# Statistics of one token tile moved from VectorE to ScalarE, and two copies halved between the engines, at the start of a layer-norm, state-space and gated-unit kernel

## The chip, the cores and the metric

One NeuronCore of a Trainium2 chip. The metric is device microseconds of one execution, median over the executions of a kernel. The span in a trace is about 1.9 us shorter than that time.

## The reference, cut to what matters

```python
def _layernorm(x, axis=-1, eps=1e-5):
    m = jnp.mean(x, axis=axis, keepdims=True)
    v = jnp.var(x, axis=axis, keepdims=True)
    return (x - m) / jnp.sqrt(v + eps)
...
    x  = A_x                      # 1 x 2048 x 576, bf16
    xn = _layernorm(x, axis=-1)
    return x + _A_ref(xn, ...) + _B_ref(xn, B_w_gate, B_w_up, B_w_down)
# _B_ref: (sigmoid(xn @ w_gate) * (xn @ w_up)) @ w_down, 576 -> 4608 -> 576
# _A_ref: a diagonal complex state space over the 2048 tokens
```

## The kernel before

Tokens are processed in tiles of 128 (tile 0, 1, 2, ...), four tiles to a block of 512. Nothing can be multiplied until the first tiles are normalised and transposed, so the start is a chain across all engines. For a tile: VectorE takes statistics of its two halves and aggregates them, ScalarE takes the square root, VectorE the reciprocal and the normalisation, TensorE 18 transposes into PSUM (where TensorE leaves its results), and ScalarE and VectorE copy the result out (9 chunks of 128 columns) into `xT`. Then the first gate/up group `start_groups[0]` can run on tiles 0 and 1, before tiles 2 and 3 are transposed.

```python
    busy(10, TB)               # warm-up matmuls on zeros, 512 columns
    busy(6, P)                 # and 128 columns
    ...
    for tt in range(2):
        ln_stats(tt)                                   # VectorE: 2 halves + aggregate
        ln_std(0, tt, tt + 1)                          # ScalarE: square root
    for tt in range(2):
        ln_recip(0, tt, tt + 1)                        # VectorE
        ln_norm(tt, twice=False)                       # VectorE
        start_transpose(tt)                            # TensorE
    consts_transpose(ptrs[1][:, NH, :])
    busy(18, P)
    start_copy(0, slice(0, NH), nc.scalar.copy)
    ln_stats(2)
    start_copy(1, slice(0, 5), nc.scalar.copy)
    ln_std(0, 2, 3)
    ln_stats(3)
    ln_std(0, 3, 4)
    start_copy(1, slice(5, NH), nc.vector.tensor_copy)
    for tt in range(2, TT_B):
        ln_recip(0, tt, tt + 1)
        ln_norm(tt, twice=False)
    start_groups[0].mms(slice(0, 2 * P))               # TensorE: tiles 0 and 1
    start_transpose(2)
    start_transpose(3)
    start_groups[1].mms(slice(0, 2 * P))               # from here on TensorE never waits
    # ... copies of tiles 2 and 3, second halves of both groups, then the steady loop
```

The order of these lines is the order of instructions on each engine. In the traces here every engine takes its own in that order: in e4 and e12 below TensorE stands for one instruction while the work of later ones is ready.

## Time and profile before

| | before |
|---|---|
| time, median of 3 (lowest to highest) | 506.17 us (506.12 to 506.29) |
| time of the execution that was profiled | 506.76 us, span 504.9 |
| first statistics of tile 0 start (tile 0 has landed) | 3.49 us |
| first transpose, tile 0 | 6.27 us |
| first gate/up group | 9.03 us |
| transposes of tile 2 | 10.29 us |
| steady stream starts | 11.45 us |

The positions are starts read from the trace. From the order of time on ScalarE and VectorE (start, duration, engine, line, operation, what it writes and reads, and in brackets the idle time before it and what ended it):

```profile
7.26 1.71 ACT L783 COPY xT<-ptr 128x1152 bf16<-128x1152 bf16 x2 [1.46 <-PE ptr L780]
```
```profile
8.20 0.21 DVE L231 BATCH_NORM_AGGREGATE mv<-bnst 128x2 f32<-128x12 f32 x1
9.01 0.42 DVE L783 COPY xT<-ptr 128x512 bf16<-128x512 bf16 x1 [0.60 <-ACT xT L783]
```

ScalarE's two copies one after the other take 1.71 us; VectorE has finished the statistics of tile 3 and waits 0.60 us for them. The change goes after that wait.

### The profile page before, as it was taken

The page shows a single profiled execution, that of the slowest core. Times are in us where ns is not written, and L with a number is a line of the kernel's source. Part 1 is how long each engine was busy: PE and PEld are TensorE (multiplying, and loading weights), DVE is VectorE, ACT ScalarE, POOL GpSimd, SP SyncE. Part 2 cuts the span into 40 slices and gives each one's busy share as a digit, 9 for nine tenths or more (in the row PEclk, how much of TensorE's full clock was granted, in tenths as well). Part 3 has the DMA queues.
Part 4 walks back from the last instruction along what each step waited for, and adds up shares of the span by engine and source line. Part 5 has one row for each costly group of instructions (what it writes and reads, how often), then busy time and mean ns, then how long its engine had stood idle before and what let it go on. Part 6 is the DMA issues. An engine that isn't in the chain of part 4 may idle for free.

```text
span 504.9 us, 13370 instructions
## 1 busy us (share of the span) xinstructions
PE 500.5 (99%) x5892; PEld 290.6 (58%) x5892; DVE 323.3 (64%) x706; ACT 204.7 (41%) x368; POOL 91.0 (18%) x134
## 2 busy tenths in 40 slices
PE   8999999999999999999999999999999999999997
PEld 6544675444477444467764444774444774446775
DVE  5889698887878687886688767696675222221111
ACT  4955733556500756530016655005655005553000
POOL 7116320123100043110001231100431001300000
PEclk9999999999999999999999999999999999999999
DMA  8997595055220099340340651200643201600001
GB/s 210 208 176 232 135 197 100 18 149 139 49 50 26 1 160 215 73 95 26 90 101 4 162 142 49 49 25 1 165 106 84 50 25 34 179 1 1 26 25 49
DMA packets 40960, 45.77 MB, mean 91 GB/s; under 512 B 28614, under 2 KB 32326, under 8 KB 40902
## 3 DMA queue, kind: packets, MB, share of 16 engines
q0 software_dynamic: 10608, 34.22, 27.8%
q1 hardware_dynamic: 29862, 10.37, 11.1%
q8 instruction: 46, 0.75, 0.6%
q10 hardware_dynamic: 432, 0.33, 0.2%
q14 instruction: 12, 0.10, 0.1%
HBM read 34.36 MB, written 2.36 MB: 73 GB/s over the span
## 4 chain that ended last, share of the span: by engine, by line
PE 99%; DVE 0%; ACT 0%; issue 0%
PE pgu L502 55%; PE pd L616 33%; PE pbu L531 7%; PE pd L576 1%; PE pd L584 1%; PE pgu L772 1%; PE ptr L780 0%; ACT xT L783 0%; DVE xn L255 0%; DVE xT L783 0%; DVE ob L585 0%; DVE warm L182 0%; DVE rstd L238 0%; DVE eps_t L178 0%; DVE zero_t L180 0%
## 5 line engine op out<-in xcount | busy, mean ns | idle before, releaser
L502 PE MATMUL pgu<-xT,wgu 64*128 64x512 bf16 (+1 forms) x2628 | 283.7, 373 | 0.1
L502 PEld LDWEIGHTS <-wgu 64*128 64x128 bf16 x2628 | 128.1, 94 | 150.4
L616 PE MATMUL pd<-wd,hT 64*128 64x288 bf16 x2208 | 140.5, 283 | 0.0
L508 ACT ACTIVATE sT<-pgu 128x512 bf16<-128x512 f32 x144 | 86.3, 600 | 120.5 <-PE pgu L502 119.6
L616 PEld LDWEIGHTS <-hT 64*128 64x128 bf16 x2208 | 107.6, 94 | 28.7
L511 DVE TENSOR_TENSOR hT<-sT,uT 128x512 bf16<-128x512 bf16 x144 | 60.6, 422 | 91.5 <-ACT uT L509 91.3
L509 ACT CAST uT<-pgu 128x512 bf16<-128x512 f32 x144 | 84.0, 583 | 0.0
L154 POOL DMA_DIRECT2D wgu<-in_B_w_gate_dram x36 | 27.6, 766 | 227.7 <-PE pgu L502 216.3
L537 ACT COPY bure<-pbu 128x512 f32<-128x512 f32 x16 | 9.4, 585 | 89.9 <-PE pbu L531 76.0
L160 POOL DMA_DIRECT2D wd<-in_B_w_down_dram x36 | 26.3, 733 | 104.9 <-PE pd L616 104.7
L627 DVE TENSOR_TENSOR acc<-acc,pd 128x576 f32<-128x576 f32 x32 | 22.7, 750 | 30.2 <-PE pd L616 30.2
L624 DVE TENSOR_TENSOR ob<-acc,pd 128x576 bf16<-128x576 f32 x14 | 9.9, 750 | 38.3 <-PE pd L616 38.3
L531 PE MATMUL pbu<-xT,bt 64*128 64x512 bf16 x288 | 33.7, 376 | 0.0
L616 PE MATMUL pd<-ctim,hst 64*128 64x288 bf16 x224 | 28.6, 283 | 0.0
L616 PE MATMUL pd<-ctre,hst 64*128 64x288 bf16 x224 | 28.6, 283 | 0.0
L616 PEld LDWEIGHTS <-hst 64*128 64x128 bf16 x504 | 24.5, 94 | 6.3
L154 POOL DMA_DIRECT2D wgu<-in_B_w_up_dram x36 | 26.5, 736 | 1.5 <-DMA wgu<-in_B_w_up_dram 1.5
L445 DVE TENSOR_TENSOR_SCAN gre<-r,g0re,wrim 128x512 bf16<-128x512 f32 x20 | 25.5, 1277 | 0.1
L531 PEld LDWEIGHTS <-bt 64*128 64x128 bf16 x288 | 14.0, 94 | 16.5
L452 DVE TENSOR_TENSOR_SCAN gim<-r,g0im,wrim 128x512 bf16<-128x512 f32 x16 | 20.4, 1275 | 0.0
L230 DVE BATCH_NORM_STATS2 bnst<-xt 128x6 f32<-128x288 bf16 x32 | 12.5, 432 | 2.3 <-DMA xt<-in_A_x_dram 2.3
L432 DVE TENSOR_TENSOR tq<-T,buim 128x512 bf16<-128x512 bf16 x20 | 13.7, 684 | 0.0
(126 smaller groups left out, 294.6 us busy)
## 6 DMA issues: line engine op xcount, KB each, us to landing
wgu<-in_B_w_gate_dram POOLq DMA_DIRECT2D x36, 288.0 KB, 4.2
wgu<-in_B_w_up_dram POOLq DMA_DIRECT2D x36, 288.0 KB, 4.8
wd<-in_B_w_down_dram POOLq DMA_DIRECT2D x36, 288.0 KB, 4.7
out_dram<-ob SPq DMA_DIRECT2D x15, 144.0 KB, 1.7
xt<-in_A_x_dram SPq DMA_DIRECT2D x10, 144.0 KB, 3.9
xt<-in_A_x_dram POOLq DMA_DIRECT2D x4, 144.0 KB, 6.8
bt<-ctre POOLq DMA_DIRECT2D x2, 288.0 KB, 6.0
bt<-ctim POOLq DMA_DIRECT2D x2, 288.0 KB, 7.7
```

The source lines that it names most:

```text
L154: eng.dma_start(w[rows, :, :], src[:, fs].rearrange("(c p) f -> p c f", p=H))
L160: nc.gpsimd.dma_start(wd[:], B_w_down[f0:f0 + FP * P, :].rearrange("(n p) d -> p n d", p=P))
L432: nc.vector.tensor_mul(tq[:], t2, b[:])
L445: nc.vector.tensor_tensor_scan(gre[:], r_bc, w[:, 0, :], g0re[:, col], ALU.mult, ALU.add)
L452: nc.vector.tensor_tensor_scan(gim[:], r_bc, w[:, 1, :], g0im[:, col], ALU.mult, ALU.add)
L502: nc.tensor.matmul(self.ps[:, gi, cols], w[rows, c, fs], xT[self.nb][rows, c, cols], start=c == 0, stop=c == NH - 1)
L508: nc.scalar.activation(sT[:], self.ps[:, 0, :], ACT.Sigmoid)
L509: nc.scalar.copy(uT[:], self.ps[:, 1, :])
L511: nc.vector.tensor_mul(h[:], sT[:], uT[:])
L531: nc.tensor.matmul(out, w, xT[self.nb][rows, c, ts_], start=c == 0, stop=c == NH - 1)
L616: m = nc.tensor.matmul(pds[k][:, a, 0:DH], lhsT[rows, :], rhs[rows, a * DH:(a + 1) * DH], start=turn == 0 and i == 0, stop=turn == 1 and i ...
L627: nc.vector.tensor_add(halves(acc[:]), halves(acc[:]), pd[:, :, 0:DH])
```

## The change

Its intent: take the statistics of tile 1 off VectorE, so that tiles 0, 2 and 3 come earlier there, and divide the copies of tiles 0 and 1 so that they overlap. The two runs of short warm-up matmuls are cut too, from 6 to 3 and from 18 to 6. ScalarE gets the mean from one accumulating pass (Identity, scale 1/576) and the variance from a second (Square of mean minus x); the second pass gives a sum, so the square root takes it with a scale of 1/576. Cuts in the diff are marked "...".

```diff
-    busy(6, P)
+    busy(3, P)
@@
+    m1, v1 = (mvs_of(0)[:, 1, i:i + 1] for i in range(2))
+    junk = [...]                                   # two scratch tiles
+    nc.scalar.activation(junk[1][:, 0:1], eps_t[:], ACT.Sqrt, ...)      # loads the table early
+    ln_stats(0)
+    nc.scalar.activation(junk[0][:], xts[1][:], ACT.Identity, bias=zero_t[:], scale=1.0 / D, accum_out=m1)
+    ln_std(0, 0, 1)
+    nc.scalar.activation(junk[1][:], xts[1][:], ACT.Square, bias=m1, scale=-1.0, accum_out=v1)
+    nc.scalar.activation(rstds[0][:, 1:2], v1, ACT.Sqrt, bias=eps_t[:], scale=1.0 / D)
+    ln_bn(2, 0)                                    # first half of tile 2's statistics
+    ln_recip(0, 0, 1)
+    ln_norm(0, twice=False)
+    start_transpose(0)
+    ln_bn(2, 1)
+    ln_recip(0, 1, 2)
+    ln_norm(1, twice=False)
+    start_transpose(1)
+    consts_transpose(ptrs[1][:, NH, :])
+    busy(6, P)
+    ln_aggr(2)
+    ln_bn(3, 0)
     for tt in range(2):
-        ... (the old order, shown above)
-    busy(18, P)
-    ...
+        start_copy(tt, slice(0, 4), nc.scalar.copy)
+        start_copy(tt, slice(4, NH), nc.vector.tensor_copy)
     ln_std(0, 2, 3)
-    ln_stats(3)
+    ln_bn(3, 1)                                    # behind the copies
+    ln_aggr(3)
     ln_std(0, 3, 4)
-    start_copy(1, slice(5, NH), nc.vector.tensor_copy)
     for tt in range(2, TT_B):
         ln_recip(0, tt, tt + 1)
         ln_norm(tt, twice=False)
```

`ln_bn` and `ln_aggr` are the two parts of `ln_stats`; nothing after these lines is changed.

More of the change, by code (lines that the diff above doesn't have):

```diff
@@ L220, with mvs_of, ln_bn, ln_aggr @@
     ln_count = [0]
-    def ln_stats(tt):
-        nb, tl = divmod(tt, TT_B)
-        if tl == 0:
+    bnst = {}
+    def mvs_of(nb):
+        if nb not in mvs:
             mvs[nb] = lnp.tile([P, TT_B, nc.vector.BN_AGGR_DIM], FP32, name="mv")
             rstds[nb] = lnp.tile([P, TT_B], FP32, name="rstd")
-        xt = xts[tt]
-        st = lnp.tile([P, 2, BN], FP32, name="bnst")
+        return mvs[nb]
+    def ln_bn(tt, gi):
+        if gi == 0:
+            bnst[tt] = lnp.tile([P, 2, BN], FP32, name="bnst")
+        nc.vector.bn_stats(bnst[tt][:, gi, :], xts[tt][:, gi * DH:(gi + 1) * DH])
+    def ln_aggr(tt):
+        nb, tl = divmod(tt, TT_B)
+        nc.vector.bn_aggr(mvs_of(nb)[:, tl, :], bnst[tt][:])
+    def ln_stats(tt):
         for gi in range(2):
-            nc.vector.bn_stats(st[:, gi, :], xt[:, gi * DH:(gi + 1) * DH])
-        nc.vector.bn_aggr(mvs[nb][:, tl, :], st[:])
+            ln_bn(tt, gi)
+        ln_aggr(tt)
     def ln_std(nb, t0, t1):
@@ L783, in start_copy @@
         eng(xT_tile(0)[:, cs, tt * P:(tt + 1) * P], ptrs[tt % 2][:, cs, :])
-    for tt in range(2):
-        ln_stats(tt)
-        ln_std(0, tt, tt + 1)
-    for tt in range(2):
-        ln_recip(0, tt, tt + 1)
-        ln_norm(tt, twice=False)
-        start_transpose(tt)
-    consts_transpose(ptrs[1][:, NH, :])
-    busy(18, P)
-    start_copy(0, slice(0, NH), nc.scalar.copy)
-    ln_stats(2)
-    start_copy(1, slice(0, 5), nc.scalar.copy)
+    m1, v1 = (mvs_of(0)[:, 1, i:i + 1] for i in range(2))
+    junk = [ssmp.tile([P, D], BF16, name="junk", tag="tq", bufs=2) for _ in range(2)]
+    nc.scalar.activation(junk[1][:, 0:1], eps_t[:], ACT.Sqrt, bias=zero_t[:], scale=1.0)
+    ln_stats(0)
[15 more added lines that the diff above has]
+    ln_bn(3, 0)
+    for tt in range(2):
+        start_copy(tt, slice(0, 4), nc.scalar.copy)
+        start_copy(tt, slice(4, NH), nc.vector.tensor_copy)
     ln_std(0, 2, 3)
-    ln_stats(3)
+    ln_bn(3, 1)
+    ln_aggr(3)
     ln_std(0, 3, 4)
-    start_copy(1, slice(5, NH), nc.vector.tensor_copy)
     for tt in range(2, TT_B):
```

## The prediction

> **What bounds the kernel now**
>
> I read the page first, for the engine that sets the end.
>
> ```profile
> PE 500.5 (99%) x5892; PEld 290.6 (58%) x5892; DVE 323.3 (64%) x706; ACT 204.7 (41%) x368; POOL 91.0 (18%) x134
> ...
> PE 99%; DVE 0%; ACT 0%; issue 0%
> ...
> L502 PE MATMUL pgu<-xT,wgu 64*128 64x512 bf16 (+1 forms) x2628 | 283.7, 373 | 0.1
> ...
> L616 PE MATMUL pd<-wd,hT 64*128 64x288 bf16 x2208 | 140.5, 283 | 0.0
> ```
>
> TensorE is the chain that ends last, and its two large groups sat idle 0.1 and 0.0 us. From the first steady gate/up matmuls on, nothing but TensorE counts: a change in the first 12 us is worth exactly the time by which that stream starts earlier, in a span of 504.9 us. So the second view is the chain cut to the first 32 us.
>
> ```profile
> 1.25 5.09 PE pgu L772 x16
> 6.34 0.90 PE ptr L780 x16
> 7.24 0.02 issue
> 7.26 1.72 ACT xT L783 x2
> 8.99 0.02 issue
> 9.01 0.42 DVE xT L783
> 9.44 0.08 DVE rstd L238
> 9.52 0.03 issue
> 9.54 0.71 DVE xn L255
> 10.25 0.04 issue
> 10.29 1.23 PE ptr L780 x36
> 11.52 20.53 PE pgu L502 x215
> ```
>
> Read downwards: warm-up matmuls until 6.3, the transposes of tiles 0 and 1, two ScalarE copies, the VectorE copy of the rest of tile 1, then reciprocal and normalisation of **tile 2**, whose end (10.24) releases the transposes of tiles 2 and 3 at 10.29. After that TensorE never waits. So two things matter: when the copies of tiles 0 and 1 are done (9.0 to 9.4), and when tile 2 is normalised (10.24). The second is the last gate, because the first gate/up group (18 matmuls from 9.03, over by 10.03) ends before it. The third view is VectorE's and GpSimd's order of time around that gate.
>
> ```profile
> 4.34 0.21 DVE L231 BATCH_NORM_AGGREGATE mv<-bnst 128x2 f32<-128x12 f32 x1
> 4.47 0.77 DVE L230 BATCH_NORM_STATS2 bnst<-xt 128x6 f32<-128x288 bf16 x2
> ...
> 5.54 0.43 DVE L255 TENSOR_SCALAR xn<-xt,mv,rstd 128x576 bf16<-128x576 bf16 x1
> ...
> 9.39 0.73 POOL L154 DMA_DIRECT2D wgu<-in_B_w_gate_dram  x1 [0.49 <-DMA wgu<-in_B_w_gate_dram]
> 9.54 0.69 DVE L255 TENSOR_SCALAR xn<-xt,mv,rstd 128x576 bf16<-128x576 bf16 x1
> 10.16 0.14 DVE L238 RECIPROCAL rstd<-rstd 128x1 f32<-128x1 f32 x1
> 10.34 0.43 DVE L255 TENSOR_SCALAR xn<-xt,mv,rstd 128x576 bf16<-128x576 bf16 x1
> ```
>
> The same normalisation takes 0.43 us three times and 0.69 once: for tile 2, exactly while GpSimd issues a weight load (9.39 to 10.13).
>
> **What the Trainium skill says**
>
> - "SBUF — State Buffer", Who interferes with whom: VectorE in a two-port mode and GpSimd share a port pair under an exclusive lock, and the one that issues first holds it. The trace agrees: the normalisation begun 0.15 us after the GpSimd issue ends 0.11 us after it and takes 0.27 us longer; in four slow VectorE instructions later in the trace (line 330, 0.59 to 0.70 us against 0.43) it is the same, and one begun before GpSimd's issue kept its 0.43.
> - "PSUM — Partial Sum Buffer", PSUM bank collisions: two engines must not read one bank at once. A transposed tile's chunks 0 to 7 fill 2 KB, one bank, so ScalarE's and VectorE's copies of one tile go one after the other. The trace agrees: VectorE's copies of tile 1, 2 and 3 each begin 0.02 us after ScalarE's of the same tile.
> - "ScalarE: Activation LUTs", What ACT_TABLE_LOAD costs: an ACTIVATE with a pointer bias takes 280 ns + 0.833 ns an element, a load about 1.28 us. The trace has 0.29 us for one element and 1.28 for each load. I use it for 576 elements: 0.76 us.
> - "TensorE: Matmul & The Clock Gate", Part 1: half clock until a window of activity has passed. The trace's clock record turns to full at 6.85 us; the transposes' pairs start 107 ns apart before it and 56 ns after.
>
> **The change part by part**
>
> 1. *Warm-up cut from 6 to 3 short matmuls.* In the half-clock part they start 0.107 us apart, so the first transpose can start at 6.27 - 3 x 0.107 = 5.95. Tile 0's normalised rows must be there: the trace has them at 5.98 now. In the change VectorE does statistics of tile 0 (ends 4.55), one half of tile 2, then waits for the unchanged square root (4.59 to 4.88), reciprocal 4.91, normalisation 5.06 to 5.49. So warm-up still binds, and transposes of tile 0 run 5.95 to 6.88, 0.32 earlier, nearly all at half clock.
>
> 2. *Tile 1's statistics on ScalarE.* Off VectorE go two half-tile statistics and an aggregate: its next tile's statistics start 0.93 us after tile 1's (5.40 against 4.47 in step). On ScalarE: first pass starts when tile 1 has landed (3.30), 0.76 us, an accumulator read of perhaps 0.2 (my estimate, from the 0.21 us of the shortest ACTIVATE in this trace, 128x5), so 4.3, before the square root of tile 0 is due at 4.59. Second pass 4.79 to 5.55, read until 5.7, square root 5.72 to 6.03, reciprocal and normalisation on VectorE end near 6.68. TensorE wants tile 1 at 6.88. So tile 1 is just in time, with 0.2 us to spare. Its transposes end 0.17 earlier than now: they start at 6.88 where they now start at 7.06.
>
> 3. *Copies halved.* Now: ScalarE copies tile 0 whole (1.12 us), then 5 chunks of tile 1 (0.70), then VectorE 4 chunks. In the change: ScalarE 4 chunks of tile 0, 7.09 to 7.68 (512 elements, 0.59); VectorE its 5 chunks 7.70 to 8.19 (0.425 + 128 more elements at the slope between its durations, 0.49); meanwhile ScalarE 4 chunks of tile 1, from the end of the constants' transposes (now 7.87, then 7.70) to 8.31; VectorE 5 chunks 8.33 to 8.82. The first gate/up group can start at 8.35 instead of 9.03: **0.68 earlier**. Its weights landed at 7.87 in the trace, so no DMA takes the wait's place.
>
> 4. *What reaches the last gate.* VectorE after its last copy no longer goes straight to tile 2's reciprocal. The change puts the second half of tile 3's statistics and its aggregate in between: copy starts 8.33, statistics 8.74, aggregate 9.22 (a half to its aggregate is 0.48 in step now), reciprocal 9.35, normalisation 9.49. Now it is 9.54. Of the 0.68 only **0.05 us** is left at this place, because 0.60 us of work (0.48 + 0.13) that VectorE did during its idle 0.60 us before 9.01 has been moved behind the copy.
>
> 5. *The port.* GpSimd's issue at 9.39 waits on a DMA that the change doesn't touch, so it should stay. If the normalisation at 9.49 is locked out, it ends at 10.24 as now, and the gain is 0.0. If it gets the port, for it comes 0.10 after the issue, not 0.15, it ends at 9.93, transposes of tile 2 start at 9.98, and the gain is 10.29 - 9.98 = **0.31 us**. Tile 3 is not in the way: its square root ends at 9.76, its normalisation at 10.45, and its transposes are due at 10.48.
>
> Everything after shifts as a whole: weight loads for the third group pair land 2.8 us before their use (19.4 against 22.2), and ScalarE's table loads (12.3 to 20.1) keep about 1 us before TensorE needs a PSUM buffer back at 22.2. Sum: 0.0 or 0.31 us, 506.17 - 0.31 = 505.86 or 506.17.
>
> **The rivals**
>
> - *The port lock keeps the whole gain* (506.1 to 506.2). For it: 9.49 lies inside 9.39 to 10.13, and 0.69 us now in the same place. Against: the trace has nothing between 0.07 us before and 0.15 us after an issue of this weight load, and one two-port instruction begun 0.25 us after an issue of another load was not held. I give it 0.4.
> - *All of the 0.68 arrives* (505.5). It needs normalisation of tile 2 before 9.0; that speaks against VectorE's new order. It would take chips on which my durations are all too long. 0.05.
> - *ScalarE's accumulating passes are slower than I think.* Then tile 1 comes late and the copies slip. But a slip up to 0.5 us still puts the normalisation inside the locked stretch and ends it at 10.24, so this costs nothing until it is past about 0.6 us. So it moves chances to the first rival more than above 506.2.
> - *The clock is granted a window later*, since fewer warm-up matmuls stand before 6.85 and transposes may count less. Windows of 3.4 us put the next grant at 10.26; the first group would take 1.9 instead of 1.0 us, and the time would be 506.7 to 507. Before the grant the window has matmuls until 5.81 instead of 6.13, thus 70% rather than 79% of it. 0.08.
> - *Another table load*, if one of the two new functions were not in the loaded table: 1.28 us or 2.57 on ScalarE before tile 1, about 506.8 to 508. The dummy square root at the start is there to load once; 0.03.
>
> **Range and chances**
>
> The gain or its absence is a few tenths of a microsecond, 0.06% of the time. A 2% change would need 10 us; the whole phase before the steady stream is 11.5 us. The before-runs spread over 0.17 us. I weigh 505.86 with one half, 506.15 with 0.4 and what is above with the rest, and put the point between the first two: 505.96 us. Range 505.5 to 506.45: at the low end more of the 0.68 arrives, at the high end a late clock or chip-to-chip noise.
>
> **What would show it**
>
> Step 1: first transpose at 5.95. Step 2: square root of tile 1 ends near 6.03, second ScalarE passes at 0.76 us, one table load before 12 us. Step 3: gate/up group at 8.35 and VectorE's last copy of tile 1 at 8.33. Step 4: tile 2's normalisation starts near 9.49. Step 5: it takes 0.43 (gain 0.3) or about 0.7 (none); transposes of tile 2 at 9.98 or 10.29. The prediction is wrong if those transposes start before 9.7 or after 10.5, or if TensorE waits anew after 12 us.

## The result, and the profile after

506.61 us, median of 6 (506.35 to 507.16), against 506.23 of before in its 6 runs (505.96 to 506.42). Ratios are the mean time of one kernel's runs over that of the other's of the same rounds, so not quite the ratio of the medians: 1.0009, with an interval of 0.9996 to 1.0021. Within 2% it is the same, as foretold; but the point lies above the foretold range of 505.5 to 506.45.

The changed kernel's page, the engines of its chain and the first group of part 5:

```profile
PE 98%; DVE 1%; DMA 1%; ACT 0%; issue 0%
...
L513 PE MATMUL pgu<-xT,wgu 64*128 64x512 bf16 (+1 forms) x2628 | 283.8, 373 | 0.2 <-ACT xT L794 0.2
```

TensorE is still 98% of the chain; its 0.2 us of idle time before gate/up groups is at the very start. The first 12 us of the chain of the changed kernel (start, length, what):

```profile
3.75 0.83 DVE bnst L233 x2
...
5.15 0.77 ACT junk L803 x2
...
6.95 0.69 PE ptr L791 x18
...
7.81 0.59 ACT xT L794
...
8.43 0.49 DVE xT L794
8.92 0.38 DVE bnst L233
...
9.32 0.21 DVE mv L237
...
9.59 0.44 DVE xn L266
...
10.08 1.23 PE ptr L791 x36
```

Before, this chain began with TensorE's warm-up; now it begins with the landing of tile 0 and runs through VectorE, ScalarE's second pass, tile 1, the copies, and then the part to look at: after the copy at 8.43 come half a tile's statistics (8.92), an aggregate (9.32), and only then the reciprocal and normalisation of tile 2 (9.59). Its transposes start at 10.08.

ScalarE of the changed kernel, its second pass:

```profile
5.05 0.76 ACT L803 ACTIVATE junk<-xt,mv 128x576 bf16<-128x576 bf16 x1
5.72 0.19 ACT L803 ACTIVATION_READ_ACCUMULATOR junk<-xt,mv 128x1 f32 x1
```

The first pass has the same two instructions, 0.77 and 0.19 us. Both take what was foretold. VectorE of the changed kernel around its copies:

```profile
7.25 0.47 DVE L794 COPY xT<-ptr 128x640 bf16<-128x640 bf16 x1
8.43 0.49 DVE L794 COPY xT<-ptr 128x640 bf16<-128x640 bf16 x1 [0.71 <-ACT xT L794]
```

It still waits, 0.71 us, between its two copies; the 0.6 us of statistics come after that idle time.

So in the two traces tile 2's transposes are 0.21 us earlier (10.08 for 10.29), and the profiled executions agree: 506.55 for 506.76. The medians say the opposite. That is what the experiments had to clear up.

### The profile page after: what moved, and what is told of

The parts are those of the page before. It is cut to its first block, busy times and chain, and to the rows that moved or that the text cites. A ratio compares the mean times of both kernels' runs of the same rounds, so it can differ in the third digit from the quotient of the medians.

```text
span 504.7 us, 13344 instructions
## 1 busy us (share of the span) xinstructions
PE 498.7 (99%) x5877; PEld 288.8 (57%) x5877; DVE 322.7 (64%) x704; ACT 206.1 (41%) x373; POOL 91.4 (18%) x134
## 4 chain that ended last, share of the span: by engine, by line
PE 98%; DVE 1%; DMA 1%; ACT 0%; issue 0%
PE pgu L513 55%; PE pd L627 33%; PE pbu L542 7%; PE pd L587 1%; PE pd L595 1%; DMA xt<-in_A_x_dram 1%; PE ptr L791 0%; DVE bnst L233 0%; DVE xn L266 0%; ACT junk L803 0%; ACT xT L794 0%; DVE xT L794 0%; DVE mv L237 0%; ACT rstd L804 0%; ACT rstd L245 0%
## 5 line engine op out<-in xcount | busy, mean ns | idle before, releaser
L442 DVE TENSOR_TENSOR wrim<-T,bure 128x512 bf16<-128x512 bf16 x20 | 13.7, 684 | 0.0
```

Of the source, the lines that this page charges most:

```text
L442: nc.vector.tensor_mul(w, t1, a[:])
```

## The experiments

Two theories stood at this point. **Theory A:** the trace of before is of an unusually late start, and the typical one is earlier than the changed kernel's. **Theory B:** the trace of before is typical, and the change loses something after 12 us. All kernels gave correct results. Times are medians, "before" is before in the same rounds.

### 1. Before and the changed kernel again, and two parts alone

e1 and e2 are the two kernels unchanged.

> The kernel before once more, unchanged. Theory A (the profile of before was a late-clock execution: full clock from 6.85 us, 506.76 us against 506.2 timed): here, with a clock granted before 6 us, the transposes of tile 2 start at 9.4 to 9.8 instead of 10.29, and normalisation of tile 2 (then begun near 9.0, ahead of GpSimd's weight load at 9.4) takes 0.43 us. Theory B (the profile of before was typical, the loss of the change comes after 12 us): they start at 10.2 to 10.4 again. Time within 0.3 us of the other runs of before either way.

> The changed kernel once more, unchanged. Its first profile had full clock from 4.06 us and tile 2's transposes at 10.08. Theory A: whatever the clock does, 9.8 to 10.1, since VectorE's and ScalarE's chain sets it and not the warm-up; 0.2 to 0.5 us slower than before. Theory B: same start, but an idle time of TensorE after 12 us that before lacks.

e3 is before with `busy(6, P)` made `busy(3, P)` and `busy(18, P)` made `busy(6, P)`, nothing else.

> Before with the shorter warm-up alone (3 and 6 small matmuls for 6 and 18). Prediction's step 1 (warm-up binds the first transposes): 0.3 us faster than before. Theory A: with an early clock the warm-up is over before tile 0 is normalised, so 0.0 (within 0.1), tile 0's transposes at tile 0's normalisation, 6.0.

e4 is the changed kernel with

```diff
     ln_std(0, 2, 3)
+    ln_recip(0, 2, 3)
+    ln_norm(2, twice=False)
     ln_bn(3, 1)
     ln_aggr(3)
     ln_std(0, 3, 4)
-    for tt in range(2, TT_B):
-        ln_recip(0, tt, tt + 1)
-        ln_norm(tt, twice=False)
+    ln_recip(0, 3, 4)
+    ln_norm(3, twice=False)
```

> The changed kernel with reciprocal and normalisation of tile 2 put ahead of the second half of tile 3's statistics and its aggregate. Prediction's step 4 and theory A (0.6 us of statistics stand before the last gate): tile 2's transposes 0.5 to 0.6 us earlier than in the changed kernel, at about 9.4, time 0.4 to 0.6 lower, so at or 0.1 to 0.2 below before. Theory B: no change.

Measured, before 506.19 us (506.05 to 506.38): e1 506.23, e2 506.37 (506.18 to 506.52), e3 506.24, e4 506.99 (506.97 to 507.21).

e1 lay between the theories: transposes of tile 2 at 10.02, clock full from 6.64. The normalisation that had taken 0.69 us took 0.43: it began at 9.44, ahead of GpSimd's weight load at 9.51, where in the first trace the load came first (9.39). So the 0.69 was an accident of that trace. Theory B fell at e2: from 12 to 500 us the view of waits has no entry for TensorE in the traces of before, the changed kernel and e2, and from the start of tile 2's transposes to the end the profiled executions of the two kernels take the same time (e1 506.46 - 10.02 = 496.44; before 506.76 - 10.29 = 496.47; changed 506.55 - 10.08 = 496.47; e2 506.18 - 9.73 = 496.45). The start alone decides.

e3 is a hit for theory A in the median: the warm-up alone is worth nothing, 506.24 for 506.19. Its trace does not show why. Its clock turned late (6.75), and even so the first transpose came when tile 0 was normalised (6.07) and tile 2's transposes 6.44 us after tile 0's first statistics; e1, with the long warm-up and the clock at 6.64, has 6.41. So with a late clock too the 0.32 us foretold for the shorter warm-up did not reach tile 2.

e4 is a miss, and it taught something. VectorE of e4:

```profile
8.98 0.43 DVE L266 TENSOR_SCALAR xn<-xt,mv,rstd 128x576 bf16<-128x576 bf16 x1
...
10.38 0.16 DVE L249 RECIPROCAL rstd<-rstd 128x1 f32<-128x1 f32 x1 [0.36 <-ACT rstd L245]
10.58 0.43 DVE L266 TENSOR_SCALAR xn<-xt,mv,rstd 128x576 bf16<-128x576 bf16 x1
```

Normalisation of tile 2 moved up as expected (8.98, which is 5.33 us after tile 0's statistics began, for 5.84 in the changed kernel) and its transposes started when the first group ended, 9.58. But tile 3 now waits for its statistics and for ScalarE's square root (0.36 us idle), is normalised at 10.58, and TensorE, in order, stands until 11.07 for it. The steady stream started at 11.69. The statistics have to be done **before** VectorE's last copy, not merely after tile 2.

### 2. The statistics into the idle time, and the two halves of the change alone

e5 is the changed kernel with `ln_bn(3, 1)` and `ln_aggr(3)` put between the copies of tile 0 and those of tile 1, into VectorE's 0.71 us:

```diff
-    for tt in range(2):
-        start_copy(tt, slice(0, 4), nc.scalar.copy)
-        start_copy(tt, slice(4, NH), nc.vector.tensor_copy)
+    start_copy(0, slice(0, 4), nc.scalar.copy)
+    start_copy(0, slice(4, NH), nc.vector.tensor_copy)
+    ln_bn(3, 1)
+    ln_aggr(3)
+    start_copy(1, slice(0, 4), nc.scalar.copy)
+    start_copy(1, slice(4, NH), nc.vector.tensor_copy)
     ln_std(0, 2, 3)
-    ln_bn(3, 1)
-    ln_aggr(3)
     ln_std(0, 3, 4)
```

> The changed kernel with the second half of tile 3's statistics and its aggregate moved from behind VectorE's copies into its 0.71 us of idle time between the two. If those 0.6 us behind the copy are what loses the gain of the earlier first group: normalisation of tile 2 starts 0.6 earlier, both tiles are ready when the first group ends, so tile 2's transposes start at the group's end, 0.4 us earlier than in the changed kernel against tile 0's landing (5.9 us after it, not 6.32), and the time is 0.3 to 0.5 below the changed kernel's, 505.9 to 506.1. If the loss lies elsewhere (after 12 us, or in ScalarE's passes): no change.

e6 is the changed kernel with the copies divided as of old (ScalarE 9 chunks and 5, VectorE the last 4):

> The changed kernel with the old division of the copies (ScalarE 9 chunks of tile 0 and 5 of tile 1, VectorE 4 of tile 1). ScalarE's copy of tile 1 waits for its transposes and the constants' in either, so I expect the first group 0.1 us later and tile 2's transposes at most 0.1 later than in the changed kernel: time equal within 0.15. The prediction's part 3 would have it 0.3 or more slower.

e7 is before with the copies halved (the loop over `start_copy` of the change after `ln_stats(2)`, then `ln_stats(3)`):

> Before with the copies halved alone, statistics of all tiles on VectorE, those of tile 3 behind the copies as in the change. The 0.93 us of tile 3's statistics then stand before tile 2's normalisation: it starts near 9.9 instead of 9.4, tile 2's transposes at 10.4 instead of 10.0, time 0.3 to 0.5 us above before. If halving is a gain by itself: 0.2 to 0.4 below.

> Before once more, for another trace of it; the two so far had full clock from 6.85 and 6.64 us and tile 2's transposes at 10.29 and 10.02. If a clock granted before 5.7 comes up: first transposes at tile 0's normalisation (about 2.4 us after tile 0 has landed), and tile 2's transposes at 9.5 to 9.8, span 504.1 to 504.4. If late again: 10.0 to 10.3.

Measured, before 506.25 (506.10 to 506.76): e5 506.15 (505.88 to 506.57), e6 506.62 (506.54 to 506.90), e7 506.68 (506.52 to 507.14), e8 506.25.

e5 did what it should: in its trace tile 2's transposes start at 9.71, 5.87 us after tile 0's first statistics (3.84), and directly behind the first group. The changed kernel has 6.33 for that. VectorE of this order, from its second trace (e11, below): the statistics now fill the time between the two copies, of which only 0.10 us stays idle.

```profile
7.01 0.47 DVE L794 COPY xT<-ptr 128x640 bf16<-128x640 bf16 x1
7.41 0.45 DVE L233 BATCH_NORM_STATS2 bnst<-xt 128x6 f32<-128x288 bf16 x1
7.89 0.21 DVE L237 BATCH_NORM_AGGREGATE mv<-bnst 128x2 f32<-128x12 f32 x1
8.20 0.49 DVE L794 COPY xT<-ptr 128x640 bf16<-128x640 bf16 x1
```

e7's time came as expected: with 0.9 us of statistics behind the copies, half of the change alone is 0.4 us slower than before (ratio 1.0009, interval 0.9997 to 1.0022). Its positions are 0.2 us earlier than expected (normalisation of tile 2 at 9.70 for 9.9, transposes at 10.18 for 10.4). In its chain:

```profile
8.17 0.49 DVE xT L783
8.66 0.73 DVE bnst L230 x2
...
9.70 0.44 DVE xn L255
```

e6's time, 506.62, is that of the changed kernel (506.61 and 506.37 in other rounds), but its trace missed: tile 2's transposes at 10.17, 6.72 after the first statistics, not 6.4. Its clock came late (6.31), so the transposes of tile 0 ended late, and ScalarE's two long copies (6.84 to 8.55) then set the first group. What the halved copies are worth by themselves stays open: this trace has a late clock, none of the changed kernel has one, and the changed kernel was not timed in e6's rounds.

e8 brought neither of its two cases but a third bound. Its clock turned at 6.23 and its first transpose waited for tile 0's normalisation (6.38), but then the first weights came late. Its chain of waits:

```profile
2.34 6.84 DMA wgu<-in_B_w_up_dram
...
9.22 1.15 PE pgu L502 x17
```

The first weights landed at 9.17 us (7.87 to 8.50 in the other thirteen traces), later than the first group could have started, and held it. A start earlier than before's 8.9 is exposed to that; the changed kernel's first group starts at 8.10 to 8.45, and in e2 the weights landed at 8.10, just as it started.

### 3. An early clock in before, and the better version

e9, e10 and e11 repeat before, the changed kernel and e5; e12 is e5 with `consts_transpose` moved from behind tile 1's transposes to between tile 0's and tile 1's.

> Before a fourth time, for a trace with an early clock. My account by now: an execution's time is the start of the steady gate/up stream plus 495.3 us, and in before that start is, with an early clock, 7.3 us after tile 0's landing (tile 2's transposes 6.15 to 6.2 after it), with a late one fixed by the warm-up (first transpose at 6.27, tile 2's at 10.0 or later). So early: tile 2's transposes at 9.6 to 9.9; late: 10.0 to 10.3.

> The changed kernel a third time. By the same account tile 2's transposes start 6.32 to 6.36 us after tile 0's landing whatever the clock (6.35 in both traces so far), and the time is 0.1 to 0.5 us above before of the same rounds. A rival: the first series of the changed kernel (506.61) was chance, and it is within 0.1 of before.

> The version with tile 3's statistics in VectorE's idle time, once more: tile 2's transposes 5.9 us after tile 0's landing, or 1.17 after the first weights if those land late; 0.3 to 0.5 us below the changed kernel and 0.1 to 0.3 below before.

> The same, and the constants' transposes moved into TensorE's idle time between tiles 0 and 1, so that ScalarE's copy of tile 1 no longer waits for them: first group 0.13 us earlier, tile 2's transposes 5.75 us after tile 0's landing, time 0.1 below the previous version, unless the first weights (8.0 to 8.5, 9.2 once) land later than that, which then holds the first group.

Measured, before 506.42 (506.16 to 506.64): e9 506.09 (506.05 to 506.72), e10 506.54 (506.40 to 506.69), e11 506.07 (505.83 to 506.35), e12 506.08 (505.95 to 506.13).

e9 had what was wanted, full clock from 4.34 us. Its chain of waits:

```profile
3.79 0.83 DVE bnst L230 x2
...
5.85 0.49 DVE xn L255
...
6.38 1.23 PE ptr L780 x36
...
7.74 1.11 PE pgu L772 x18
...
8.88 1.16 PE pgu L502 x18
10.04 1.13 PE ptr L780 x36
```

Compare it with the chain in the prediction: no warm-up at the head, tile 0's normalisation releases the first transpose, and the first group and tile 2's transposes follow on TensorE without a gap. (The 18 matmuls at 7.74 are the second warm-up. They end at 8.85, and ScalarE's copies, over at 8.82, would have held the first group almost as long.) Tile 2's transposes start at 9.97, and that is 6.18 us after the first statistics, though tile 0 came 0.30 later than in the first trace of before. All of these traces side by side, with positions counted from the start of tile 0's first statistics:

| kernel (trace) | full clock from | first statistics | + first transpose | + first group | + tile 2's transposes | us of this execution |
|---|---|---|---|---|---|---|
| before, the one predicted from | 6.85 | 3.49 | 2.78 | 5.54 | **6.80** | 506.76 |
| before, e1 | 6.64 | 3.61 | 2.66 | 5.32 | 6.41 | 506.46 |
| before, e9 | 4.34 | 3.79 | 2.59 | 5.09 | **6.18** | 506.40 |
| changed | 4.06 | 3.75 | 2.11 | 4.70 | 6.33 | 506.55 |
| changed, e2 | 4.6 to 5.0 | 3.41 | 2.12 | 4.69 | 6.32 | 506.18 |
| changed, e10 | 5.45 | 3.51 | 2.35 | 4.74 | 6.37 | 506.41 |
| changed + e5's order, e5 | 4.6 to 4.9 | 3.84 | 2.11 | 4.70 | 5.87 | 506.15 |
| changed + e5's order, e11 | 4.70 | 3.52 | 2.11 | 4.69 | **5.87** | 505.83 |

(The traces of e2 and e5 hold no record of the clock; I give the two warm-up matmuls between which their spacing falls. e8 is left out, for its weights set it.) The changed kernel's 6.32 to 6.37 hardly moves over turns from 4.06 to 5.45; no trace shows it with a turn after 6, so that it would not move then is not shown. Before's goes from 6.18 to 6.80, and that is not the clock alone: 0.17 of it is the slow normalisation of tile 2 in the first trace (worked out below). e10's first transpose is 0.23 later than the others' because the change put half of tile 2's statistics ahead of tile 0's reciprocal on VectorE, and tile 2 landed only at 4.77 in that trace; the later waits took it up but for 0.05.

All executions together: before 48 of them, median 506.25 (505.96 to 506.76); changed 16, median 506.52 (506.18 to 507.16); e5, e11 and e12 15, median 506.08 (505.83 to 506.57). In each of its three series the changed kernel's mean is above that of before (0.43, 0.17 and 0.14 us), and the ratios are 1.0009, 1.0004 and 1.0003, though every interval holds 1. So it is most likely about 0.25 us slower, 0.05% of the time.

An estimate ties this to the traces: 496.45 us and a first statistics at 3.60, the mean of all fourteen traces, give 506.23 for before with e9's 6.18, 506.46 with e1's 6.41, and 506.39 for the changed kernel with 6.34. Before's median of 506.25 thus fits an early clock. But its four profiled executions took 506.76, 506.46, 506.70 and 506.40, each above the median of its series (506.23, 506.23, 506.25 and 506.09). So no trace shows a typical execution of before, and that its clock is mostly early is argued, not shown.

e5's order beats the changed kernel by about 0.4 (in the rounds that timed both, e11 and e10, the medians are 506.07 and 506.54, and the slowest of its executions, 506.35, is faster than the fastest of the changed kernel, 506.40) and before by 0.1 to 0.35 (ratios 0.9999, 0.9995 and 0.9993; intervals that hold 1 too).

e12 missed its extra 0.1: TensorE stood for the constants.

```profile
6.86 0.20 PE L196 MATMUL ptr<-ident,crows 27*64 27x27 bf16 x2 [0.53 <-DMA crows<-in_A_Lambda_im_dram]
6.99 0.69 PE L791 MATMUL ptr<-ident,xn 128*64 128x128 bf16 x18
```

In this trace those transfers of 1.1 KB landed too late for a place this early; tile 1's transposes, in order behind them, started at 6.99 instead of 6.71, and tile 2's 6.01 us after the first statistics for 5.87. The old place of the constants was not slack, it covered a DMA.

## Why the prediction was wrong

The verdict, no change of 2%, was right; the point and its range were not, and the sign was most likely wrong too: 506.17 - 0.2 was foretold, and the change measured 0.14 to 0.43 us slower in the mean of each of its three series, though each interval holds no difference as well.

- **The step that failed is the last line of "The change part by part": "506.17 - 0.31 = 505.86 or 506.17".** It takes a gain counted against positions in a trace and subtracts it from a median to which this trace doesn't belong: its own execution took 506.76. The positions themselves were good. Foretold for tile 2's transposes: 9.98 or 10.29. Measured: 10.08, 9.73 and 9.88. With the 496.45 us that an execution takes from there, 9.98 and 10.29 make 506.43 and 506.74, and the medians measured were 506.61, 506.37 and 506.54. The arithmetic belonged to 506.76 - 0.31. Part of the agreement is luck: counted from tile 0's first statistics, 9.98 and 10.29 are 6.49 and 6.80, and the three traces have 6.33, 6.32 and 6.37; in the first of them tile 0 came 0.26 us later than in before's trace.
- Behind it stands "So warm-up still binds", read from that one trace. The clock's turn lay at 3.95 to 6.85 us in the twelve traces that record it. In e9, at 4.34, the first warm-up binds nothing in before: its first transpose comes 2.59 us after the first statistics for 2.78, its first group 2.50 after that for 2.76, and tile 2's transposes 1.09 later for 1.26; these 0.19, 0.26 and 0.17 are the 0.62 between 6.80 and 6.18. The first two go with the clock: the warm-up ends earlier, and the transposes of tile 0 run at full clock (tile 1's start 0.53 us after tile 0's in e9, 0.79 in the first trace). In the changed kernel the first transpose waited for tile 0's normalisation (5.86, 5.53 and 5.86); the foretold 5.95, behind the warm-up, came only in e6, with its clock at 6.31. The rival "the clock is granted a window later" was thought of for the changed kernel only. That before's trace had such a late turn itself was not asked. How often timed executions of before have a late clock is open, as they leave no trace.
- "The second is the last gate" also held in that trace alone. Without the slow normalisation the first group would have released tile 2's transposes at 10.12 (9.03 + 1.09, the time from the first group to them in e1 and e9), so the slow normalisation cost 0.17. In e1, e8 and e9 the first group is the last gate of before.
- "What reaches the last gate", that 0.60 us moved behind the copy takes back nearly all of the first group's gain, was right in kind and size. Against e9 the changed kernel is 0.48 ahead at the first transpose (2.11 for 2.59), 0.39 at the first group, and 0.15 **behind** at tile 2 (6.33 for 6.18): 0.54 is lost between the two. e5 and e11, which move only those two instructions, get 0.46 of it back (5.87).
- The port (0.4 of the chances) was not what decided in the changed kernel. GpSimd's load came at 10.08 in the changed trace, after the normalisation at 9.59, which took 0.43. In before the lock was met in one trace of four. The prediction's guess that a normalisation begun soon enough after the load is not held fits e6: begun 0.03 us after the load at 9.66, tile 2's took 0.43. "GpSimd's issue at 9.39 waits on a DMA that the change doesn't touch, so it should stay" failed: that issue came at 9.39 in before's first trace and at 10.08 in the changed kernel's.
- "Its weights landed at 7.87 in the trace, so no DMA takes the wait's place" rested on one trace as well. In the changed trace they landed at 8.36, 0.1 us before the group; e8's 9.17 would have held it.
- Right: the two passes with 0.76 us and 0.19 for the read (0.2 foretold), one table load before 12 us, tile 1's square root over at 6.23 (6.03 foretold, with tile 0 landing 0.26 later), the first group 0.6 earlier (9.03 to 8.45; 0.68 foretold), and from VectorE's last copy to tile 2's normalisation every start just 0.10 later than foretold (8.33, 8.74, 9.22, 9.49 became 8.43, 8.84, 9.32, 9.59); nothing new after 12 us.
- The range was too narrow as well: "The before-runs spread over 0.17 us" is the spread of three runs, and 48 spread over 0.80. The chances given add up to 1.06, and no gain is 506.17 in one place and 506.15 in another; neither slip moves the point by more than hundredths.

## What to carry to other kernels

Before subtracting a gain from a median, put the profiled execution's own time beside that median: if they differ by more than the gain, the trace shows another case than the timing measures, and what differs (here the turn of TensorE's clock, a port, a landing) has to be known first. In a chain of in-order engines, work that filled an engine's idle time costs most of its length once it is moved behind the instruction that this time was spent waiting for (here 0.46 us of 0.60, by e5 and e11); look for the idle time that the change leaves elsewhere (0.71 us between the two copies) and put it there. A gate can be two: freeing tile 2 alone made tile 3 the gate, and the time worse by 0.6 us.

## What the Trainium skill lacked or had wrong

- "ScalarE: Activation LUTs" says that an ACTIVATE can give an accumulator output, but not what it costs. In the changed kernel the accumulator is read by an instruction of its own, 0.18 to 0.19 us, after a pass whose 0.76 us fit the page's 280 ns + 0.833 ns an element. The read starts 0.09 us before the pass is over (5.72 against 5.05 + 0.76), so that it adds 0.10.
- "TensorE: Matmul & The Clock Gate", Parts 1 and 4: it puts the turn to full clock after about 3.4 us of sustained activity. In the changed kernel's trace and in e7's it came 2.8 and 2.7 us after the first matmul (1.25 to 4.06 and 3.95); the page's word that the window runs freely fits the scatter up to 6.85 (5.6 us after the first matmul). It also says that full clock doesn't engage for transposes; here pairs of them start 107 ns apart before the turn and 56 ns after it, like the matmuls.
- "SBUF — State Buffer", Who interferes with whom, does not say how soon after its issue GpSimd has the shared ports. Normalisations begun 0.03, 0.05 and 0.07 us after a weight load (e6's of tile 2, the changed kernel's and e2's of tile 3) kept their 0.43 us; the one begun 0.15 us after it, in before, took 0.69.
